# Attention and two expert layers on one core: transposes and the last queries' scores through two row halves of the array, operands without shifted columns

## The chip, the cores and the metric

The kernel runs on one core of a Trainium2 chip. The metric is the device time of one execution in microseconds (us), the median of the runs. The core has a matrix engine (TensorE; PE in the profile, and PEld for its weight loads), VectorE (DVE), ScalarE (ACT), GpSimd (POOL) and a sync engine whose queue (SP) issues all DMAs. TensorE reads SBUF and writes PSUM banks of 512 float32 columns.

## What is computed

```python
def _attn_ref(q, k, v):                       # (4, 8, 576, 64) each: 32 heads
    q_rot, k_rot = (rotate(q), rotate(k))     # rotary tables cos, sin over 576 positions
    scores = scale * np.matmul(q_rot, k_rot.transpose(0, 1, 3, 2))
...
    attn = np.exp(scores)
    attn = attn / (np.sum(attn, axis=-1, keepdims=True) + 1e-09)
    return np.matmul(attn, v).astype(np.float32)
...
    h = x @ w_in                              # layer 1: (2304, 512) @ (512, 2048), float64 weights
    g = P / (Q + 1e-06)                       # a rational function of h
    return (g @ w_out).astype(np.float32)
...
    h = np.maximum(x @ w_in, 0.0)             # layer 2
    return (h * h @ w_out).astype(np.float32)
```

## The kernel before

**Two stages.** The attention works on 16 pairs of heads; the two heads of a pair lie in the two halves of the 128 partitions (64 features each). The two expert layers follow (3840 matrix products of 464 or 456 columns). Nearly every product is made of three float32r products (high by high, low by high, high by low), for precision.

**One pair of heads.** `rope` loads q and k with their swapped halves (`raw`), multiplies by the tables, adds (POOL, for the first pairs DVE), splits into a high part (`hi`, a cast on ACT) and a low part (`lo`, POOL). `scores` computes, for each of five groups of queries (c = 0 to 4; four of 128 and a last one of 64 for each head), products of 64 rows: head 0 in the upper row half of the array, head 1 in the lower one, side by side, into two PSUM banks `sc`. DVE takes the scaled maximum and moves the scores to `e` (one instruction, "max" below), ACT does the exponential. TensorE transposes `e` in pieces of 128 x 128 (`move`; 41 in a pair) into one of two PSUM banks `tr`, alternately; ACT or DVE copies them to `et` ("eth"). `av` multiplies `et` by v with 64 output columns for each head, the heads in the two column halves of the array, in float32 (each product stands as two instructions in the trace), for the queries of c = 0, 1 (256 columns) and c = 2, 3, 4 (320). DVE copies the result to `t`; `normalise` forms the reciprocal sums, sends them through DRAM (`dr`, `rr`), and POOL multiplies (`fin`).

Before the change every q and k operand has 640 columns (`W`), head 0 shifted by 64: in this layout the last 64 queries of both heads make one product of full height with `qt` (four small ACT casts, "wrap", build it), so its scores come in one bank and one max.

**The order.** All work is recorded as tasks with an engine, an estimated duration, a rank and its reads and writes. `Plan.run` deals them out: on each engine it takes, of the tasks that are ready by its estimates, the one with the lowest rank (the position in the program plus an entry of the table `RANK`). The result is a fixed order of instructions on each engine, and each engine executes its own in order, waiting on semaphores. TensorE tasks carry a mode, rows, columns or full, by the part of the array that they use; the planner charges a change of mode (`SWITCH`).

**Weights of the layers.** Float64 words are turned into float32 pairs by `Weights.chunk`, on DVE three instructions ("wy") for each chunk of 512 columns. Seven chunks are prepared during the attention, in the pairs from the fourth to the tenth.

Of the kernel before, what the change touches and what calls it, by code (L numbers as in the profile page):

```python
# [19 lines left out]
P = 128  # L20
B, H, S, D = 4, 8, 576, 64
NPAIR = B * H // 2
W = S + D
# [16 lines left out]
CUT = 192  # L40
KCUT = 352
# [49 lines left out]
class Plan:  # L91
# [38 lines left out]
    def run(self, trace=True):  # L130
# [41 lines left out]
SWITCH, BOND = 160, 56.5  # L172

RANK = {"const": -298.5, "load": -213.6, "rope": 80.3, "add": -79.5, "hi": 153.2, "lo": -107.5,
        "wrap": 223.7, "spread": -16.2, "vload": -129.4, "qk": -228.9, "max": -56.4, "exp": 149.9,
        "dup": 356, "tr": -129, "trc": -323.5, "eth": -52.9, "av": 224.5, "t": -2.5, "inv": 97,
        "fin": -180.1, "wload": 342.6, "wx": 198.5, "wy": 82.9, "wh": 310.7, "wl": -189.1, "xh": 498.3,
        "xl": 83.4, "h": -171.3, "chain": 19.2, "gh": -121.9, "gl": 471.2, "o": 216.6, "evac": 21.5,
        "out": -157}
# [55 lines left out]
class Attention(Ops):  # L235


    def __init__(self, nc, plan, early, late, scores, banks, dram, qk, v, tables, ident, xf):
# [4 lines left out]
        self.ntr = self.ny = 0  # L243
        self.tab = early.tile([P, 2, W], F32, "tab")
        self.raw = early.tile([P, 4, W], F32, "raw")
        two = lambda shape, t: [a.tile([P] + shape, F32R, f"{t}{i}") for i, a in enumerate((early, late))]
        self.qh, self.ql, self.kh, self.kl = (two([W], t) for t in ("qh", "ql", "kh", "kl"))

        self.qt = two([2, P], "qt")
# [9 lines left out]
    def constants(self):  # L259
        for i, cols in enumerate((slice(0, KCUT), slice(KCUT, W))):  # L260
            self.dma((40 * i, "const"), self.tab[:, :, cols], self.tables_ap[:, :, cols], w=[("tab", i)], ns=900)
        self.dma((90, "const"), self.ident, self.ident_ap, w=["ident"])
        for i in range(2):
            for x, key in ((self.qt[i][0:64, :, 64:128], ("zero", i, 0)), (self.qt[i][64:128, :, 0:64], ("zero", i, 1))):
                self.fill("pool", 200, (20, "const"), f(x), 0.0, r=["early"], w=[key])

    def rotate(self, p, j, cols, pieces, rank, eng, r=()):

        raw, n = self.raw, cols.stop - cols.start
        two, w = slice(2 * j, 2 * j + 2), [("raw", j, i) for i in pieces]  # L270
        self.tt(eng[0], 2 * n, (rank, "rope"), raw[:, two, cols], raw[:, two, cols], self.tab[:, :, cols], ALU.mult,
                r=[("tab", 0), ("tab", 1)][cols.start >= KCUT:2 if cols.stop > KCUT else 1] + ["early", *r], w=w)
        self.tt(eng[1], n, (rank, "add"), raw[:, 2 * j, cols], raw[:, 2 * j, cols], raw[:, 2 * j + 1, cols], ALU.add,
                r=["early"], w=w)

    def rope(self, p):
# [3 lines left out]
        up, dn = slice(0, 64), slice(64, 128)  # L280

        def prepare(j, cols, pieces, rank):

            n = cols.stop - cols.start
            first = p == 0
# [3 lines left out]
            engines = {0: ("dve", "dve") if j else ("pool", "pool"), 1: ("dve", "dve")}.get(p, ("pool", "pool"))  # L289
            self.rotate(p, j, cols, pieces, rank, engines)  # L290
            src = raw[:, 2 * j, cols]
            self.hi("act", n, (rank, "hi"), hi[:, cols], src, r, wh)
# [3 lines left out]
        if p == 0:  # L296
            prepare(1, slice(0, KCUT), (0,), at - 50)
            prepare(0, slice(0, CUT), (0,), at - 40)
            prepare(1, slice(KCUT, W), (1,), at - 30)
            prepare(0, slice(CUT, W), (1,), at - 9)  # L300
        else:
            prepare(0, slice(0, W), (0, 1), at)
            prepare(1, slice(0, W), (0, 1), at + KFIRST)
        for i, part in enumerate(parts[0]):
            for rows, dst in ((up, slice(0, 64)), (dn, slice(64, 128))):
                self.act(64, (at, "wrap"), self.qt[b][rows, i, dst], f(part[rows, S:W]), r=["early", (names[0][i], b, 1)],
                         w=[("qt", b, i, rows.start)], sb=True)
        self.dma((at, "vload"), self.vst[b], self.v[p], r=["early"], w=[("v", b)])

    def hi(self, eng, n, rank, out, src, r, w):  # L310
        if eng == "act":
            self.act(n, rank, out, src, r=r + ["early"], w=w, sb=True)
        else:
            self.ts("dve", n, rank, out, src, 1.0, None, ALU.mult, r=r + ["early"], w=w)

    def scores(self, p, c):

        b, n = p % 2, 9 * p + 2 * c
        qh, ql, kh, kl, qt = (x[b] for x in (self.qh, self.ql, self.kh, self.kl, self.qt))
        rd = [(x, b, i) for x in ("kh", "kl") for i in range(2)] + ["early", "scores"]  # L320
        if c == 4:
            rd += [("zero", b, i) for i in range(2)] + [("qt", b, i, j) for i in range(2) for j in (0, 64)]
            jobs = [(0, slice(0, P), [(qt[:, 0], kh), (qt[:, 1], kh), (qt[:, 0], kl)])]
        else:
            at = slice(128 * c + 64, 128 * c + 192)
            rd += [(x, b, i) for x in ("qh", "ql") for i in range(2) if p or (i == 0 and c == 0) or (i == 1 and at.stop > CUT)]

            jobs = [(h, slice(64 * h, 64 * h + 64), [(qh[:, at], kh), (ql[:, at], kh), (qh[:, at], kl)]) for h in range(2)]

        def product():  # L330
            for i in range(3):
                for j in range(2):
                    for h, rows, terms in jobs:
                        w, k = terms[i]
                        first = (0 if c < 4 and h else 64) + 288 * j
                        self.mm(self.sc[h][:, j, 0:288], w[rows], k[rows, first:first + 288], i == 0, i == 2)

        self.pe(6 * 131, (n, "qk"), product, r=rd, w=[("sc", h) for h, _, _ in jobs], mode="full" if c == 4 else "rows")

    def unit(self, p, u):  # L340
        n = 9 * p + u
        b = p % 2
        c, h = divmod(u, 2)
        slot = (5 * p + c) % NE
        e, sc = self.e[slot], self.sc[h]
        if h == 0:
            self.scores(p, c)
        if u == 0:
            self.fill("pool", 70, (n - 1, "qk"), self.sums[b], 1.0, w=[("sums", b)])
        col = 5 * h + c if u < 8 else 4  # L350
        neg, sums = self.neg[b][:, col:col + 1], self.sums[b][:, col:col + 1]

        self.ts("dve", 2 * 288, (n, "max"), e[:, h].rearrange("p (j k) -> p j k", j=2), sc[:, :, 0:288], -SCALE, None,
                ALU.mult, op1=ALU.min, accum_out=neg, ns=760, ps=True, r=[("sc", h), "scores"], w=[("neg", b, col), ("e", slot, h)])
        self.act(S, (n, "exp"), e[:, h], e[:, h], func=AF.Exp, sb=True, bias=neg, scale=-1.0, accum_out=sums,
                 r=[("neg", b, col), ("sums", b)], w=[("e", slot, h), ("sum", b, col)])
        if u == 8:
            self.act(64, (n, "dup"), e[:, 1, 0:64], e[:, 0, 512:576], r=[("e", slot, 0)], w=[("e", slot, 1)], sb=True)

        part = 0 if c < 2 else 1  # L360
        cols = slice(128 * (c % 2), 128 * (c % 2) + 128)
        self.move([(e[:, h, 128 * k + 64 * h:128 * k + 64 * h + 128], k) for k in range(4)], (n, "tr"), [("e", slot, h)],
                  [((lambda t: t), lambda z: z[:, 4 * h:4 * h + 4, cols], 512, (part, "m", u))] if u < 8 else
                  [((lambda t: t.rearrange("p k (h q) -> p k h q", h=2)),
                    lambda z: z[:, 0:8, 256:320].rearrange("p (h k) q -> p k h q", h=2), 512, (1, "m", 8))], p, part)
        mid = lambda s: self.e[s].rearrange("p h k -> p (h k)")[:, 512:640]
        if u in (3, 7):
            prev = (slot + NE - 1) % NE
            self.move([(mid(prev), 0), (mid(slot), 1)], (n, "trc"), [("e", x, y) for x in (prev, slot) for y in (0, 1)],
                      [((lambda t: t[:, 0:2]), lambda z: z[:, 8, 0:256].rearrange("p (c q) -> p c q", c=2), 256, (part, "c"))], p, part)  # L370
        if u == 8:
            self.move([(mid(slot), 0)], (n, "trc"), [("e", slot, 0), ("e", slot, 1)],
                      [((lambda t, s=s: t[s, 0, s]), lambda z, s=s: z[s, 8, 256:320], 64, (1, "d", s.start))
                       for s in (slice(0, 64), slice(64, 128))], p, 1)

    def move(self, blocks, at, r, outs, p, part):
        i = self.ntr % len(self.tr)
        self.ntr += 1
# [7 lines left out]
        for src, dst, n, key in outs:  # L386
# [340 lines left out]
```

## Time and profile before

| | |
|---|---|
| median of 3 runs | 1102.25 us (1099.67 to 1103.45) |
| the profiled execution | 1099.96 us, span 1098.2 us |
| attention, to the first product of the layers | about 280 us |
| PE busy, share of the span | 1071.5 us, 98% |
| DVE / ACT / POOL busy | 786.8 (72%) / 644.3 (59%) / 554.5 us (50%) |
| chain that ended last | PE 94%, DVE 3%, ACT 1% |

A busy PE is not PE at its peak: ends of products are modelled and overlap. Whether PE sets the pace is read from the chain, and what a product costs from the distance of the starts of equal products.

### The profile page before, as it was taken

What the parts mean: (1) busy time and instruction counts of PE and PEld (TensorE: products, weight loads), DVE (VectorE), ACT (ScalarE), POOL (GpSimd) and SP (SyncE); (2) the same over time, 40 slices, a digit from 0 to 9 for tenths busy, and PEclk for the clock granted to TensorE, in tenths of its full rate; (3) what the DMA queues carried; (4) which work ended last, traced back from release to release, by engine and by line L of the source; (5) the groups of instructions that cost most, each with busy time, mean ns of one, the idle gap of its engine ahead of it and who ended that gap; (6) DMA issues with size and microseconds to landing.
All of it is one profiled execution on the core that took longest, in us unless ns stands there. A gap on an engine that the chain in (4) does not pass through costs nothing.

```text
span 1098.2 us, 16333 instructions
## 1 busy us (share of the span) xinstructions
PE 1071.5 (98%) x6000; PEld 900.2 (82%) x6000; DVE 786.8 (72%) x1439; ACT 644.3 (59%) x1283; POOL 554.5 (50%) x435
## 2 busy tenths in 40 slices
PE   4999999999799999999999999999999999999998
PEld 3666666666588888888888888888888888888887
DVE  6789888777898879988998999753254447435334
ACT  4888988787767877676676776453352234223221
POOL 3889999881478868876777776220020012001000
PEclk9999999999999999999999999999999999999999
DMA  4364554431001112101111100231031013000002
GB/s 151 116 199 132 166 155 129 144 109 36 12 20 47 50 58 59 39 20 58 39 41 40 56 1 20 73 101 39 1 96 39 20 39 96 1 20 1 35 35 104
DMA packets 25537, 71.25 MB, mean 65 GB/s; under 512 B 5104, under 2 KB 9328, under 8 KB 25456
## 3 DMA queue, kind: packets, MB, share of 16 engines
q1 hardware_dynamic: 25456, 70.20, 20.9%
q8 instruction: 47, 0.77, 0.3%
q14 instruction: 34, 0.28, 0.1%
HBM read 65.21 MB, written 4.98 MB: 64 GB/s over the span
## 4 chain that ended last, share of the span: by engine, by line
PE 94%; DVE 3%; ACT 1%; DMA 0%; issue 0%; SPq 0%; DVEq 0%; ACTq 0%
PE bank L232 44%; PE ph L232 36%; PE bank L383 8%; PE sc L232 7%; DVE raw L208 0%; DMA raw<-in_qk 0%; DVE xl L208 0%; DVE xf L208 0%; ACT e L198 0%; DVE tt L208 0%; DVE wy L213 0%; DVE u L213 0%; ACT xh L196 0%; ACT et L196 0%; SPq L229 0%
## 5 line engine op out<-in xcount | busy, mean ns | idle before, releaser
L232 PE MATMUL ph<-xh,wsi 128*128 128x464 f32 (+1 forms) x680 | 198.5, 373 | 4.5 <-DVE g L213 4.5
L232 PE MATMUL bank<-gh,wso 128*128 128x464 f32 (+1 forms) x680 | 197.6, 372 | 0.0
L196 ACT CAST gh<-g 128x464 fp32r<-128x464 f32 (+1 forms) x160 | 91.9, 576 | 153.8 <-PE bank L232 141.1
L232 PE MATMUL ph<-xh,wli 128*128 128x464 f32 (+1 forms) x600 | 174.2, 371 | 0.1
L232 PE MATMUL bank<-gh,wlo 128*128 128x464 f32 (+1 forms) x600 | 174.3, 371 | 0.0
L208 DVE TENSOR_TENSOR gl<-g,gh 128x464 fp32r<-128x464 f32 (+1 forms) x80 | 51.7, 647 | 142.5 <-ACT gh L196 142.4
L232 PEld LDWEIGHTS ph<-xh,wsi 128*128 128x128 f32 x680 | 128.1, 189 | 20.9 <-ACT xh L196 4.9
L232 PEld LDWEIGHTS bank<-gh,wso 128*128 128x128 f32 x680 | 127.6, 188 | 14.8 <-DVE xf L208 0.3
L218 DVE TENSOR_SCALAR_CACHE_REDUCE e<-sc 128x576 f32<-128x576 f32 x144 | 105.2, 755 | 40.4 <-PE sc L232 39.7
L232 PE MATMUL ph<-xl,wsi 128*128 128x464 f32 (+1 forms) x340 | 127.0, 374 | 1.6 <-DVE xl L208 1.5
L232 PE MATMUL bank<-gl,wso 128*128 128x464 f32 (+1 forms) x340 | 126.5, 372 | 0.0
L232 PEld LDWEIGHTS ph<-xh,wli 128*128 128x128 f32 x600 | 112.3, 188 | 14.2 <-DVE g L213 0.8
L232 PEld LDWEIGHTS bank<-gh,wlo 128*128 128x128 f32 x600 | 112.6, 188 | 12.9
L208 POOL TENSOR_TENSOR gl<-g,gh 128x464 fp32r<-128x464 f32 (+1 forms) x80 | 103.5, 1295 | 26.1 <-ACT gh L196 25.2
L198 ACT ACTIVATE e<-e,neg 128x576 f32<-128x576 f32 x144 | 111.1, 775 | 7.6 <-DVE e L218 6.9
L232 PE MATMUL bank<-gl,wlo 128*128 128x464 f32 (+1 forms) x300 | 111.6, 372 | 0.0
L232 PE MATMUL ph<-xl,wli 128*128 128x464 f32 (+1 forms) x300 | 111.4, 371 | 0.0
L208 POOL TENSOR_TENSOR u<-u,ab 128x464 f32<-128x464 f32 (+1 forms) x80 | 105.1, 1316 | 1.9
L383 PE MATMUL bank<-ident,e 128*128 128x128 f32 x656 | 98.0, 285 | 1.0 <-ACT et L196 0.8
L208 DVE TENSOR_TENSOR xf<-bank,xf 128x464 f32<-128x464 f32 (+1 forms) x120 | 74.4, 634 | 31.5 <-PE bank L232 30.0
L232 PE MATMUL bank<-et,vst 128*64 128x256 f32 (+1 forms) x640 | 96.8, 420 | 0.1
L198 ACT ACTIVATE tt<-ph 128x464 f32<-128x464 f32 (+1 forms) x80 | 44.4, 555 | 87.8 <-DVE g L208 72.5
(76 smaller groups left out, 1989.3 us busy)
## 6 DMA issues: line engine op xcount, KB each, us to landing
raw<-in_qk SPq DMA_DIRECT2D x30, 640.0 KB
rawi<-in_wi SPq DMA_DIRECT2D x32, 512.0 KB
rawo<-in_wo SPq DMA_DIRECT2D x32, 512.0 KB
vst<-in_v SPq DMA_DIRECT2D x16, 320.0 KB
rr<-dr SPq DMA_DIRECT2D x32, 144.0 KB
out<-xf SPq DMA_DIRECT2D x12, 232.0 KB
out<-xf SPq DMA_DIRECT2D x8, 228.0 KB
raw<-in_qk SPq DMA_DIRECT2D x1, 448.0 KB
```

Of the source, the lines that this page charges most:

```text
L196: self.nc.scalar.copy(ap(out), ap(src))
L198: self.nc.scalar.activation(ap(out), ap(src), func, **{k: ap(x) for k, x in kw.items()})
L208: self.plan.add(eng, ns, rank, lambda: self.engine(eng).tensor_tensor(ap(out), ap(a), ap(b), op=op), r, w, shared=not ps)
L218: self.plan.add(eng, ns, rank, lambda: self.engine(eng).tensor_scalar(ap(out), ap(a), ap(s0), ap(s1), op0=op0, **{k: ap(x) for k, x in kw. ...
L232: self.nc.tensor.matmul(ap(out), ap(w), ap(x), start=start, stop=stop)
L383: self.nc.tensor.transpose(ap(tr[:, k]), ap(src), ap(self.ident))
```

## The change

Transposes take 64 partitions of `e` at a time: the upper half goes through the upper row half of the array into the first `tr` bank, the lower half through the lower row half into the second, two at a time, each with 64 columns of the identity. Both banks belong to one `move`. The copies to `et` are split in the same way (`EVAC` puts six of eight large ones on ACT). q and k have 576 columns, `qt` and its casts are gone. The scores of the last 64 queries go through the row halves too: head 0 as a product of 64 rows by 64 columns, head 1 as one of 64 rows by 128 columns, of which the upper 64 results are used; they need both banks and two maxima of 64 partitions. `t` is copied in one piece for both heads; the reciprocals of head 1 come in two DMAs. All entries of `RANK` are new, so the order changes everywhere, in the layers too.

```diff
-CUT = 192
-KCUT = 352
+CUT = 128
+KCUT = 288
+TRANSPOSE = 60
+ROPE = {(0, 0): "pool", (0, 1): "dve", (1, 0): "dve", (1, 1): "dve"}
+EVAC = {("m", c, r): "act" for c in range(4) for r in range(2) if (c, r) not in ((1, 1), (2, 1))}
...
-SWITCH, BOND = 160, 56.5
+SWITCH, BOND = 160, 77.2
...
-        self.raw = early.tile([P, 4, W], F32, "raw")
+        self.raw = early.tile([P, 4, S], F32, "raw")
...
-            jobs = [(0, slice(0, P), [(qt[:, 0], kh), (qt[:, 1], kh), (qt[:, 0], kl)])]
...
+            at = slice(128 * c, 128 * c + 128) if c < 4 else slice(S - P, S) if h else slice(S - 64, S)
+            jobs.append((slice(64 * h, 64 * h + 64), slice(0, at.stop - at.start), [(qh[:, at], kh), (ql[:, at], kh), (qh[:, at], kl)]))
...
-        tr, et = self.tr[i], self.et[part][p % 2]
+        et = self.et[part][p % 2]
 
         def transposes():
-            for src, k in blocks:
-                self.nc.tensor.transpose(ap(tr[:, k]), ap(src), ap(self.ident))
-
-        self.pe(109.5 * len(blocks), at, transposes, r=r + ["ident"], w=[("tr", i)])
+            for k, pair in enumerate(zip(*halves)):
+                for i, src in enumerate(pair):
+                    rows = slice(64 * i, 64 * i + 64)
+                    src = ap(src)
+                    self.nc.tensor.transpose(ap(self.tr[i])[0:src.shape[1], 64 * k:64 * k + 64], src[rows], ap(self.ident)[rows, rows])
+
+        self.pe(TRANSPOSE * len(halves[0]), at, transposes, r=r + ["ident"], w=[("tr", i) for i in range(2)], mode="rows")
...
-            self.take("dve", m, (at, "t"), self.t[own, o:o + m], y[own, a:a + m], r=[yk], w=[("t", h, o)])
+        self.take("dve", n, (at, "t"), self.t[:, 256 * part:256 * part + n], y[:, 0:n], r=[yk], w=[("t", part)])
```

Two places of the new order matter below. The first is DVE at the turn from pair 12 to pair 13, before (`e<-sc` is a max, `et<-bank` a copy of transposes, `t<-bank` a copy of the product with v):

```order
L218 TENSOR_SCALAR e_93,neg_97<-sc_125 128x576
L218 TENSOR_SCALAR e_93,neg_97<-sc_126 128x576
L397 COPY et_108<-bank_65 64x64 x2
L432 STREAM_TRANSPOSE rt_104<-r_102 128x32
L218 TENSOR_SCALAR e_94,neg_97<-sc_125 128x576
L218 TENSOR_SCALAR e_94,neg_97<-sc_126 128x576
L397 COPY t<-bank_66 64x256 x2
L218 TENSOR_SCALAR e_95,neg_97<-sc_125 128x576
L218 TENSOR_SCALAR e_95,neg_97<-sc_126 128x576
```

The same turn on DVE in the changed kernel, the maxima of c = 0, of c = 1 and of c = 2:

```order
L220 TENSOR_SCALAR e_93,neg_97<-sc_123 128x576
L220 TENSOR_SCALAR e_93,neg_97<-sc_124 128x576
L385 COPY et_106<-bank_64 128x2x64
L385 COPY et_106<-bank_65 128x2x64
L385 COPY et_106<-bank_64 128x4x64
L385 COPY et_106<-bank_65 128x4x64
L385 COPY et_106<-bank_64 64x64
L220 TENSOR_SCALAR e_94,neg_97<-sc_123 128x576
L220 TENSOR_SCALAR e_94,neg_97<-sc_124 128x576
L385 COPY et_106<-bank_65 64x64
L385 COPY t<-bank_66 128x256
L220 TENSOR_SCALAR e_95,neg_97<-sc_123 128x576
```

Five copies of the pair before now stand between the maxima of c = 0 and of c = 1, where two small copies stood. In the same stretch TensorE has the scores of c = 1 and of c = 2 directly behind each other (24 products in a row, as at 12 places of the attention), and the first transposes of the pair behind them.

The second place is TensorE at the scores of the last queries, before:

```order
L383 MATMUL bank_65<-ident,e_94 128x128 x4
L232 MATMUL bank_67<-et_107,vst_121 64x320 x2
L232 MATMUL sc_125<-kh_88,qt_90 128x288 x4
L232 MATMUL sc_125<-kl_89,qt_90 128x288 x2
L383 MATMUL bank_64<-ident,e_94 128x128 x4
L383 MATMUL bank_65<-ident,e_95 128x128 x4
```

And in the changed kernel (the pair of rows with 64x288 and 128x288 comes six times, with `ql` and `kl` too):

```order
L234 MATMUL bank_67<-et_106,vst_119 64x320 x4
L372 MATMUL bank_64<-ident,e_95 128x64
L372 MATMUL bank_65<-ident,e_95 128x64
L372 MATMUL bank_64<-ident,e_92 128x64
L372 MATMUL bank_65<-ident,e_92 128x64
L234 MATMUL bank_67<-et_106,vst_119 64x320 x2
L234 MATMUL sc_123<-kh_88,qh_86 64x288
L234 MATMUL sc_124<-kh_88,qh_86 128x288
```

Six products of full height became six pairs in the row halves, and their outputs alternate between 64 and 128 partitions. Over the whole attention TensorE's order changes mode (rows, columns, full) 254 times before and 144 times after, the step into the layers included.

## Rows read from the trace of the kernel before

**Rows 1.** Busy time of each engine, attention and layers (windows).

```profile
core 0: us, PE busy (x) PEld busy (x) DVE busy (x) ACT busy (x) POOL busy (x), PEclk, DMA share, GB/s
40.00:277.00 237.00, 236.82 (x1977) 160.15 (x1977) 193.24 (x492) 197.06 (x479) 193.18 (x114) 1.00 0.44 132
300.00:1098.00 798.00, 793.65 (x3786) 709.89 (x3784) 549.07 (x868) 407.25 (x720) 331.12 (x290) 1.00 0.14 43
```

**Rows 2.** The chain that ended last, 199 to 232 us: start, length, what.

```profile
by line: PE bank L383 35.1%; PE bank L232 35.0%; PE sc L232 30.0%
...
199.74 1.66 PE bank L232 x12
201.40 0.99 PE sc L232 x12
...
215.71 1.66 PE bank L232 x12
```

**Rows 3.** Weight loads of the last queries' scores, once in each pair (timeline).

```profile
76.55 0.56 PEld L232 LDWEIGHTS sc<-kh,qt 128*128 128x128 f32 x4 [0.49 <-DVE et L397]
...
191.14 0.56 PEld L232 LDWEIGHTS sc<-kh,qt 128*128 128x128 f32 x4 [0.49 <-DVE et L397]
...
207.05 0.56 PEld L232 LDWEIGHTS sc<-kh,qt 128*128 128x128 f32 x4 [0.49 <-DVE et L397]
...
223.02 0.56 PEld L232 LDWEIGHTS sc<-kh,qt 128*128 128x128 f32 x4 [0.49 <-DVE et L397]
```

**Rows 4.** TensorE in one pair (timeline).

```profile
201.33 0.30 PEld L232 LDWEIGHTS sc<-kh,qh 64*128 64x128 f32 x4 [0.49 <-DVE t L397]
...
201.71 0.43 PE L232 MATMUL sc<-kh,ql 64*128 64x288 f32 x4
...
201.97 0.42 PE L232 MATMUL sc<-kl,qh 64*128 64x288 f32 x4
202.32 0.85 PEld L383 LDWEIGHTS bank<-ident,e 128*128 128x128 f32 x8 [0.16 <-issue]
202.32 1.09 PE L383 MATMUL bank<-ident,e 128*128 128x128 f32 x8
...
203.35 1.30 PE L232 MATMUL bank<-et,vst 128*64 128x320 f32 x8
...
206.37 0.76 PE L232 MATMUL bank<-et,vst 128*64 128x320 f32 x4
...
213.04 0.66 PE L383 MATMUL bank<-ident,e 128*128 128x128 f32 x4
```

**Rows 5.** VectorE in the same stretch (timeline).

```profile
202.43 0.76 DVE L218 TENSOR_SCALAR_CACHE_REDUCE e<-sc 128x576 f32<-128x576 f32 x1 [1.13 <-PE sc L232]
203.11 0.08 DVE L218 DVE_READ_ACCUMULATOR e<-sc 128x1 f32 x1
203.11 0.75 DVE L218 TENSOR_SCALAR_CACHE_REDUCE e<-sc 128x576 f32<-128x576 f32 x1
203.79 0.08 DVE L218 DVE_READ_ACCUMULATOR e<-sc 128x1 f32 x1
...
206.35 0.42 DVE L397 COPY et<-bank 128x256 f32<-128x256 f32 x1
...
206.69 0.75 DVE L218 TENSOR_SCALAR_CACHE_REDUCE e<-sc 128x576 f32<-128x576 f32 x1
...
212.75 0.45 DVE L397 COPY et<-bank 64x64 f32<-64x64 f32 x2
```

**Rows 6.** A wait of TensorE for DVE in the first pair (timeline).

```profile
26.93 0.08 DVE L218 DVE_READ_ACCUMULATOR e<-sc 128x1 f32 x1
...
27.07 0.98 PEld L232 LDWEIGHTS sc<-kh,qt 128*128 128x128 f32 x4 [2.41 <-DVE e L218]
```

**Rows 7.** Groups between 70 and 268 us (by line and form): busy, mean ns.

```profile
L198 ACT ACTIVATE e<-e,neg 128x576 f32<-128x576 f32 x111 | 85.7, 775 | 5.2 <-DVE e L218 4.8
...
L208 POOL TENSOR_TENSOR raw<-raw,tab 128x1280 f32<-128x1280 f32 x22 | 65.0, 2968 | 1.8 <-DMA raw<-in_qk 1.6
...
L213 DVE SCALAR_TENSOR_TENSOR wy<-wx,wy 128x512 uint32<-128x512 uint32 x7 | 5.7, 813 | 0.2
...
L218 DVE TENSOR_SCALAR wy<-rawi 128x512 uint32<-128x512 uint32 x4 | 4.5, 1132 | 0.0
...
L213 DVE SCALAR_TENSOR_TENSOR wy<-rawi,wy 128x512 uint32<-128x512 uint32 x4 | 3.7, 915 | 0.0
```

More of the change, by code (lines that the diff above doesn't have):

```diff
@@ L171 @@
 SAME, CROSS = 130, 180
-SWITCH, BOND = 160, 56.5
[L174 to L179, printed above, removed]
+SWITCH, BOND = 160, 77.2
+RANK = {"const": -332.5, "load": -240.8, "rope": 66.7, "add": -190.1, "hi": 466.7, "lo": -245, "wrap": 223.7,
+        "spread": -16.2, "vload": -62.2, "qk": 7.4, "max": -58.9, "exp": 101.9, "dup": 356, "tr": -448.9,
+        "trc": 381.9, "eth": -54.1, "av": 438, "t": 370.8, "inv": 804, "fin": -323.6, "wload": 966,
+        "wx": 467.4, "wy": 51.1, "wh": 143.9, "wl": -174.2, "xh": 554.7, "xl": 53.4, "h": -384.7,
+        "chain": -206.7, "gh": -85.2, "gl": 575.4, "o": 40.3, "evac": -273.4, "out": -182.5}
 class Ops:
@@ L259, in constants @@
     def constants(self):
-        for i, cols in enumerate((slice(0, KCUT), slice(KCUT, W))):
+        for i, cols in enumerate((slice(0, KCUT), slice(KCUT, S))):
             self.dma((40 * i, "const"), self.tab[:, :, cols], self.tables_ap[:, :, cols], w=[("tab", i)], ns=900)
         self.dma((90, "const"), self.ident, self.ident_ap, w=["ident"])
[L263 to L274, printed above, removed]
     def rope(self, p):
@@ L332, in product @@
                 for j in range(2):
-                    for h, rows, terms in jobs:
+                    for h, (rows, m, terms) in enumerate(jobs):
                         w, k = terms[i]
[L335 to L341, printed above, removed]
+                        self.mm(self.sc[h][m, j, 0:288], w[rows], k[rows, 288 * j:288 * j + 288], i == 0, i == 2)
@@ L342, in unit @@
+        self.pe(6 * 131, (n, "qk"), product, r=rd, w=[("sc", h) for h in range(2)], mode="rows")
+    def unit(self, p, c):
+        n = 9 * p + 2 * c
         b = p % 2
-        c, h = divmod(u, 2)
         slot = (5 * p + c) % NE
[L345 to L348, printed above, removed]
+        e, ek = self.e[slot], [("e", slot, h) for h in range(2)]
+        if c == 0:
             self.fill("pool", 70, (n - 1, "qk"), self.sums[b], 1.0, w=[("sums", b)])
-        col = 5 * h + c if u < 8 else 4
@@ L351, in unit @@
[L351 to L374, printed above, removed]
@@ L389, in eth @@
-    def eth(self, n, cols):
-        return "act" if cols == 512 and n % 9 not in (2, 5) else "dve"
+        self.scores(p, c)
+        every = slice(0, P)
+        for h, rows, i, col in [(0, every, 0, c), (1, every, 1, 5 + c)] if c < 4 else [(h, slice(64 * h, 64 * h + 64), 1, 4) for h in range(2)]:
+            self.ts("dve", 2 * 288, (n + h, "max"), e[rows, i].rearrange("p (j k) -> p j k", j=2), self.sc[h][rows, :, 0:288],
+                    -SCALE, None, ALU.mult, op1=ALU.min, accum_out=self.neg[b][rows, col:col + 1], ns=760, ps=True,
+                    r=[("sc", h), "scores"], w=[("neg", b, col, h), ("e", slot, h)])
+            if c < 4 or h:
+                self.act(S, (n + h, "exp"), e[:, i], e[:, i], func=AF.Exp, sb=True, bias=self.neg[b][:, col:col + 1],
+                         scale=-1.0, accum_out=self.sums[b][:, col:col + 1],
+                         r=[("neg", b, col, x) for x in (range(2) if c == 4 else (h,))] + [("sums", b)],
+                         w=[("e", slot, x) for x in (range(2) if c == 4 else (h,))] + [("sum", b, col)])
@@ new lines, in unit @@
+        part = c // 2 if c < 4 else 1
+        q = 128 * (c % 2)
+        flat = lambda s: self.e[s].rearrange("p h k -> p (h k)")
+        blocks = lambda s, i, h: [self.e[s][:, i, 128 * k + 64 * h:128 * k + 64 * h + 128] for k in range(4)]
+        mid = lambda s: flat(s)[:, 512:640]
+        prev = (slot + NE - 1) % NE
+        every8 = lambda x: x.rearrange("p (k q) -> p k q", q=64)
+        if c < 4:
+            src = blocks(slot, 0, 0) + blocks(slot, 1, 1)
+            self.move([src, src], (n + 1, "tr"), ek,
+                      [(r, every, slice(0, 512), lambda z, r=r: z[:, 0:8, q + 64 * r:q + 64 * r + 64], ("m", c, r)) for r in range(2)], p, part)
@@ new lines, in unit @@
+        mids = [(r, every, slice(0, 128), lambda z, r=r: z[:, 8, 0:256].rearrange("p (c q) -> p c q", c=2)[:, :, 64 * r:64 * r + 64],
+                 ("c", r)) for r in range(2)]
+        if c == 1:
+            both = [mid(prev), mid(slot)]
+            self.move([both, both], (n + 1, "trc"), [("e", prev, h) for h in range(2)] + ek, mids, p, part)
+        if c == 4:
+            prev2 = (slot + NE - 2) % NE
+            both = [mid(prev2), mid(prev)]
+            last = [e[:, 1, 512:576], mid(slot)]
+            own = [slice(64 * r, 64 * r + 64) for r in range(2)]
+            self.move([both + blocks(slot, 1, r) + [last[r]] for r in range(2)], (n, "trc"),
+                      [("e", s, h) for s in (prev2, prev, slot) for h in range(2)],
+                      mids + [(r, every, slice(128, 384), lambda z, r=r: z[:, 4 * r:4 * r + 4, 256:320], ("m", 4, r)) for r in range(2)] +
+                      [(r, own[r], slice(384, 448), lambda z, r=r: z[own[r], 8:9, 256:320], ("d", r)) for r in range(2)], p, 1)
@@ new lines, in move @@
+    def move(self, halves, at, r, outs, p, part):
+        et = self.et[part][p % 2]
+        def transposes():
+            for k, pair in enumerate(zip(*halves)):
[4 more added lines that the diff above has]
+        self.pe(TRANSPOSE * len(halves[0]), at, transposes, r=r + ["ident"], w=[("tr", i) for i in range(2)], mode="rows")
+        for i, rows, cols, dst, key in outs:
+            n = cols.stop - cols.start
+            self.take(EVAC.get(key, "dve"), n, (at[0], "eth"), dst(et), self.tr[i][rows, cols].rearrange("p (k q) -> p k q", q=64),
+                      r=[("tr", i)], w=[("et", p % 2, part) + key])
@@ L406, in av @@
         self.ny += 1
-        keys = [("et", b, part, "m", x) if isinstance(x, int) else ("et", b, part, "d", int(x[1:])) if x[0] == "d"
-                else ("et", b, part, "c") for x in us]
+        keys = [("m", c, r) for c in ((0, 1), (2, 3, 4))[part] for r in range(2)] + [("c", r) for r in range(2)]
+        keys = [("et", b, part) + k for k in keys + [("d", r) for r in range(2)] * part]
         def product(js):
@@ L447, in build @@
         for p in range(NPAIR):
-            for u in range(9):
-                self.unit(p, u)
-                if u == 3:
+            for c in range(5):
+                self.unit(p, c)
+                if c == 1:
                     self.av(p, 0)
@@ L626, in build @@
         ps = ctx.enter_context(tc.tile_pool(name="ps", bufs=1, space=PSUM))
-        banks = [ps.tile(s, F32, name=f"bank{i}") for i, s in enumerate([[P, 4, P]] * 2 + [[P, 512]] * 2)]
+        banks = [ps.tile([P, 512], F32, name=f"bank{i}") for i in range(4)]
         xf = base.tile([P, NDM, NT], F32, name="xf")
```

77 lines of the change are left out of this document (24 added, 53 removed).

## Prediction

> **What bounds the kernel now.** I read the windows first [rows 1]: in the attention PE is busy in all of 237 us, DVE, ACT and POOL in 193 to 197; in the layers PE is busy in 793.65 of 798 us. Since a busy PE need not be the bound, I then read the chain that ended last for two pairs of heads [rows 2]: it runs through nothing but TensorE, 35.1% transposes, 35.0% products with v, 30.0% scores. The pace of the pairs is the distance of the same weight load in neighbouring pairs [rows 3]: 223.02 - 207.05 = 15.97 us in a light pair, and (191.14 - 76.55) / 7 = 16.37 us in the seven heavy ones, in which DVE also unpacks weights. The layers' products stay as they are and leave 4 us of idle PE in 798, so only the attention and the step out of it can give anything.
>
> **What a pair costs TensorE today** [rows 4]. Eight transposes take 1.09 us and four 0.66, so one is (1.09 - 0.66) / 4 = 0.108 us; 41 make 4.4 us. Four instructions of the product with v over 320 columns, two side by side, are worth 1.30 - 0.76 = 0.54, so a pass of 320 columns is 0.27 us (0.84 ns a column); five passes of two instructions for 320 columns and for 256 (0.216 each) make 2.7 + 2.16 = 4.85. Scores: 201.97 - 201.71 = 0.26 for two pairs of row halves, 0.13 a pair of 288 columns; five groups of six make 3.9. The sum is 13.2. The pair takes 15.97; the missing 2.8 us go to some 16 changes of mode (254 in 16 pairs), 0.17 us each, which is also the idle time in front of the first weight load of the transposes [rows 4].
>
> **Part 1: the transposes.** 128 columns in 0.108 us are 0.84 ns a column, exactly the rate of the float32 product with v, so I take a transpose to be bound by its moving columns. With 64 columns it is 0.054, with the few ns between instructions 0.057 us for both halves together. That the halves run together is what the scores show: the four weight loads of two row halves start within 0.30 us, four full ones need 0.56 [rows 3, 4]. 41 steps then cost 2.3 us instead of 4.4. The bounds: 0.108 if the halves take turns or the weight load sets the pace (nothing gained), and 0.054 below.
>
> **Part 2: modes.** 144 changes instead of 254: 9 a pair, 1.5 us instead of 2.7. Scores of the last queries: six pairs at 0.13 for six full products at 0.13, nothing. So TensorE's need falls from 15.97 to about 3.9 + 2.3 + 4.85 + 1.5 = 12.6 us. If it stayed the bound, the kernel would gain 3.3 us in 16 pairs, 53 us.
>
> **Part 3: what is late next.** Both banks of `sc` now belong to every group, both banks of `tr` to every move, and DVE gets a tenth max and split copies. I walk through one light pair by the new order, with times from the rows. A max starts 1.10 us after the first weight load of its scores (201.33 to 202.43) [rows 4, 5], of which 0.11 is the load, hidden when transposes stand ahead. One max is 0.68 (202.43, 203.11, 203.79), a copy of 256 elements 0.34 (206.35 to 206.69), one of 64 about 0.24, one of 128 between, 0.27 [rows 5]. From the end of a max's read to the next weight load there are 0.06 (26.93 + 0.08 to 27.07) [rows 6], so 0.13 after the slot of the max.
>
> The scores of c = 0 start at 0. DVE takes their maxima from 0.98 to 2.35, then the five copies (2 x 0.27 + 2 x 0.34 + 0.24 = 1.46) to 3.81, and only then the maxima of c = 1, ready since 3.6, to 5.18. The scores of c = 2 wait for both banks, to 5.31. TensorE has nothing else in its order between c = 1 and c = 2: it is idle for 2 us here, and for half a microsecond ahead of c = 1. From 5.31 on it works without a gap to the next pair's c = 0: scores of c = 2 (0.90 with the load), c = 3, c = 4 (0.79 each), 34 transpose steps (1.9), products with v of 5 x 0.54 and 4 x 0.43 (4.4), 8 changes of mode (1.4), together 10.2. In this part every bank is free in time (c = 3 is wanted at 8.5, its banks are free at 7.9). The pair takes 5.3 + 10.2 = 15.5 us, 0.45 less than now. That is my reading of the change: nearly all of the 3.3 us that TensorE saves is spent on a wait for DVE at the start of each pair.
>
> The Trainium skill, "TensorEngine Tiling (Array Packing)", section "PSUM Bottleneck", says that tiling speeds up TensorE but not the copies out of PSUM, which may become the bottleneck. No row of the kernel before shows that, since TensorE sets its pace; by the rule alone the gain is the smaller one of the walk, not the 53 us.
>
> **Heavy pairs.** A chunk's three instructions are 1.13 + 0.92 + 0.81 = 2.9 us of DVE [rows 7]. Today they cost 16.37 - 15.97 = 0.4 a pair, since DVE waits for TensorE. In the new order one or two of them stand in the DVE stretch ahead of c = 2; the same walk gives 16.3 for one such pair and 16.8 for its neighbour, so I take 16.5, 0.15 more than now (bounds: 15.6, all hidden, and 18.4, all on the path).
>
> **Other engines.** ACT loses five small copies and one eth a pair and keeps its nine exponentials of 0.775 us; POOL's rotary work shrinks by a tenth (2.97 us multiplications [rows 7]). Both were at 13 of 16 us, so neither decides. The start, some 5 us of rotary work on DVE before the first products, loses a tenth, 0.5 us. The layers' new order can only lose, since PE is full there; I take 0 (bound 4, as much as they idle today).
>
> **Sum.** Nine light intervals (the first one, cold, among them) x -0.45 = -4.0; seven heavy x +0.15 = +1.0; start -0.5: -3.5, so 1096.5 us on the profiled execution's own time of 1099.96. That execution lies 0.2% below the median of 1102.25; on that the same saving is 1098.7. I say 1097. About 0.3%, 3.3 us, is what a measurement of this kernel can tell from no change, and my saving sits at that edge.
>
> **Rivals.**
> A. DVE catches up better than in my walk (copies cheaper, ACT taking its share earlier): the wait ahead of c = 2 halves, 1 us a pair, 16 us: about 1082. For it: DVE is busy in only 193 of 237 us [rows 1]. Against: its order is fixed, and the copies stand ahead of the maxima.
> B. The change doesn't do what it says: a transpose step costs 0.108, because the halves take turns. The 34 steps on the path cost 34 x 0.051 = 1.7 us more a pair, 28 us: about 1124. It decides from a step of 0.07 on (0.45 / 34 more than 0.057). For it: no row shows four instructions within 0.057 us for long. Against: the score halves.
> C. Slower by the mixed shapes of the last scores. 64 and 128 output columns alternate twelve times a pair. If each alternation costs what a change of mode costs now (0.17) and the halves no longer overlap (6 x 0.13), this is 2.8 us on the path of every pair, 45 us: about 1142. For it: from full to column halves (`bank<-ident` to `bank<-et,vst`) only the columns change, and there too the chain has its 0.17. Against: both are row-half products in one stream, and the hardware may use the full width for both. It decides from 0.04 us per alternation.
> The Trainium skill, same page, section "Key Properties", has a rule that stands for C: changing the tiling mode, not just the tile, drains TensorE. No run here shows whether 64 x 64 next to 64 x 128 counts as such a change.
> D. Heavy pairs, or the layers' new order, cost more than I take: heavy pairs at 17.5 instead of 16.5 and 2 us in the layers, 9 us: about 1106. DVE in the first layer is as full as in the attention and its order is new.
>
> **Chances.** My walk 0.50, A 0.14, B 0.10, C 0.10, D 0.16. The walk alone spans 1091 to 1103 (0.35 us a pair either way, the latencies' uncertainty), so faster by over 0.3% is A and 0.6 of the walk, 0.44; slower is B, C, D's larger part and a little of the walk, 0.30; the same 0.26. The range for 8 in 10 reaches from 1085, well into A, to 1124, B's time; C and the far side of A stay outside.
>
> **What would show it.** Right: transposes of 64 columns that start 0.057 us apart in pairs; the chain of the attention no longer all TensorE but with DVE's maxima and copies of `et` ahead of c = 1 and c = 2; weight loads of scores idle for some 2 us once a pair behind a max; light pairs 15.5 apart. Wrong in step 1: distance 0.1. Rival C: the last queries' scores of a pair take 3 us instead of 0.8. Rival D: intervals of the heavy pairs above 17, or PE idle in the layers. If pairs come 14 us apart, my walk misjudged DVE.

## The result: 0.9% slower, because the new waits let TensorE's clock fall

The changed kernel takes 1111.13 us (median of 12 runs, 1103.69 to 1115.98), the kernel before 1102.19 (12 runs); the ratio is 1.0091, 95% interval 1.0069 to 1.0113. The forecast was 1097 with "faster" as the likeliest sign. The profiled execution is the longest of the twelve, 1115.98 us, span 1114.2.

The windows of the profile after, columns as in [rows 1]: the attention, the layers, then two neighbouring light pairs (from the last queries' scores of one pair to those of the next) and a stretch of the second one.

```profile
core 0: us, PE busy (x) PEld busy (x) DVE busy (x) ACT busy (x) POOL busy (x), PEclk, DMA share, GB/s
40.00:277.00 237.00, 213.58 (x2525) 150.10 (x2521) 197.64 (x499) 165.74 (x369) 170.44 (x111) 0.92 0.39 122
300.00:1114.00 814.00, 805.97 (x3836) 720.71 (x3834) 558.09 (x893) 419.49 (x740) 341.34 (x299) 1.00 0.14 42
...
203.84:219.95 16.11, 14.34 (x185) 9.82 (x183) 13.33 (x35) 11.52 (x27) 12.35 (x8) 1.00 0.39 115
219.95:236.84 16.89, 15.62 (x184) 10.86 (x182) 13.11 (x35) 11.56 (x27) 12.29 (x8) 0.90 0.37 110
...
229.14:232.56 3.42, 3.42 (x33) 2.71 (x33) 2.34 (x8) 1.91 (x5) 3.42 (x3) 0.50 0.03 5
```

The reader is to see two things. TensorE, busy in all of the attention before [rows 1], now stands idle for 23 us of 237. And the granted clock, 1.00 there before, is 0.92: in the second pair it is 0.50 (1.2 GHz) for 3.42 us. The trace has twelve such stretches, 51 us in all, eleven of them in the attention; the kernel before has two, at its start and at the turn to the layers.

The chain that ended last, 199 to 232 us (start, length, what):

```profile
203.91 1.02 PE sc L234 x12
...
206.63 0.88 ACT e L200 x2
...
207.53 1.48 DVE r L220
...
209.04 0.36 DVE r L415
...
210.21 0.76 DVE e L220 x3
210.97 1.19 DVE et L385 x5
212.15 1.36 DVE e L220 x4
...
213.56 0.98 PE sc L234 x11
214.54 0.57 PE bank L372 x15
...
224.04 0.88 PE sc L234 x12
...
226.40 1.06 PE sc L234 x11
...
228.13 0.76 DVE e L220 x3
...
228.94 1.52 PE sc L234 x11
```

Where [rows 2] showed nothing but TensorE, the chain now leaves it. In the first of the two pairs it is away from 204.9 to 213.56: ACT's work with the exponential of the last queries, the sums' reciprocal, the maxima of c = 0, the five copies of `et`, the maxima of c = 1, then the scores of c = 2. In the second pair it is away twice for 1.5 us, for the maxima of c = 0 (224.9 to 226.40) and for those of c = 1 (227.46 to 228.94). The copies and maxima are the stretch that the forecast walked through; the reciprocal ahead of them in the first pair (L220 and L415 on `r`) is not in it.

TensorE in the first pair, and its two longest waits in the second (timeline, answers to [rows 4]):

```profile
203.84 0.55 PE L234 MATMUL sc<-kh,qh 64*64 64x288 f32 x4
...
204.41 0.50 PE L234 MATMUL sc<-kl,qh 64*64 64x288 f32 x4
...
210.34 0.40 PE L234 MATMUL sc<-kh,qh 64*128 64x288 f32 x1 [0.40 <-DVE e L220]
211.02 0.53 PE L234 MATMUL sc<-kh,qh 64*128 64x288 f32 x3 [0.28 <-DVE e L220]
...
212.88 0.39 PE L234 MATMUL sc<-kh,qh 64*128 64x288 f32 x1 [0.80 <-DVE e L220]
213.56 0.53 PE L234 MATMUL sc<-kh,qh 64*128 64x288 f32 x3 [0.29 <-DVE e L220]
...
216.27 0.71 PE L372 MATMUL bank<-ident,e 64*128 64x64 f32 x16
216.79 0.51 PE L234 MATMUL sc<-kh,qh 64*128 64x288 f32 x4
...
228.26 0.40 PE L234 MATMUL sc<-kh,qh 64*128 64x288 f32 x1 [0.81 <-DVE e L220]
228.94 0.69 PE L234 MATMUL sc<-kh,qh 64*128 64x288 f32 x3 [0.28 <-DVE e L220]
```

Eight steps of transposes take 216.79 - 216.27 = 0.52 us, 0.065 a step of two halves: forecast 0.057, before 0.108. The last queries' scores are done in 0.8 us. The waits for DVE are there, 0.40 + 0.28 ahead of c = 1 and 0.80 + 0.29 ahead of c = 2. The second pair has less of them, 0.18 and 0.81 + 0.28, yet it is the second in which the clock falls, at 229.14, right behind the last of them.

VectorE and POOL in the same place (two timelines):

```profile
207.53 1.47 DVE L220 TENSOR_SCALAR r<-sums 128x32 f32<-128x32 f32 x1 [0.38 <-ACT e L200]
209.04 0.35 DVE L415 RECIPROCAL r<-r 128x32 f32<-128x32 f32 x1
...
209.56 0.72 DVE L220 TENSOR_SCALAR_CACHE_REDUCE e<-sc 128x576 f32<-128x576 f32 x1
...
274.64 0.18 DVE L220 TENSOR_SCALAR r<-sums 128x32 f32<-128x32 f32 x1 [0.27 <-ACT e L200]
```

```profile
207.53 1.44 POOL L210 TENSOR_TENSOR kl<-raw,kh 128x576 fp32r<-128x576 f32 x1
```

The same addition to 32 sums takes 0.18 us when POOL is idle and 1.47 when it starts together with POOL's subtraction; it ends when that ends. (Before the change its mean was already 738 ns; now it is 998.) The unpacking of the weights also gets longer beside POOL. Its two slowest groups (30 to 295 us, busy and mean ns), first before, then after:

```profile
L218 DVE TENSOR_SCALAR wy<-rawo 128x512 uint32<-128x512 uint32 x3 | 3.2, 1075 | 0.0
L213 DVE SCALAR_TENSOR_TENSOR wy<-rawo,wy 128x512 uint32<-128x512 uint32 x3 | 3.1, 1018 | 0.0
```

```profile
L215 DVE SCALAR_TENSOR_TENSOR wy<-rawo,wy 128x512 uint32<-128x512 uint32 x3 | 5.8, 1931 | 0.0
L220 DVE TENSOR_SCALAR wy<-rawo 128x512 uint32<-128x512 uint32 x3 | 5.3, 1763 | 0.0
```

All `wy` instructions together take 25.3 us in the seven chunks, before 20.2. The Trainium skill, "Trainium Architecture — The Big Picture", section "What this means for kernel authors", says that DVE and GpSimd share an SBUF port under an exclusive lock; the rows of the addition agree (0.18 us alone, 1.47 beside POOL).

### The profile page after: what moved, and what is told of

Its sections match the earlier page's. It is cut to its first block, busy times and chain, and to the rows that moved or that the text cites. A ratio compares the mean times of both kernels' runs of the same rounds, so it can differ in the third digit from the quotient of the medians.

```text
span 1114.2 us, 17891 instructions
## 1 busy us (share of the span) xinstructions
PE 1061.9 (95%) x6752; PEld 901.6 (81%) x6752; DVE 794.3 (71%) x1487; ACT 621.8 (56%) x1187; POOL 535.3 (48%) x431
## 4 chain that ended last, share of the span: by engine, by line
PE 87%; DVE 8%; issue 2%; DMA 1%; ACT 1%; POOL 1%; SPq 0%; DVEq 0%; ACTq 0%; POOLq 0%
PE bank L234 42%; PE ph L234 35%; PE sc L234 6%; DVE e L220 4%; PE bank L372 3%; DVE et L385 1%; DMA raw<-in_qk 1%; DVE r L220 1%; POOL raw L210 0%; ACT e L200 0%; DVE wy L215 0%; SPq L231 0%; DMA cols<-in_b 0%; DVE xl L210 0%; POOL ql L210 0%
## 5 line engine op out<-in xcount | busy, mean ns | idle before, releaser
L220 DVE TENSOR_SCALAR_CACHE_REDUCE e<-sc 128x576 f32<-128x576 f32 (+1 forms) x160 | 115.5, 751 | 26.9 <-PE sc L234 22.7
L210 POOL TENSOR_TENSOR u<-u,ab 128x464 f32<-128x464 f32 (+1 forms) x80 | 100.1, 1254 | 3.3
L234 PE MATMUL bank<-et,vst 128*64 128x256 f32 (+1 forms) x640 | 100.4, 440 | 0.9 <-DVE et L385 0.9
L234 PE MATMUL sc<-kh,qh 64*128 64x288 f32 (+1 forms) x320 | 60.6, 379 | 37.7 <-DVE e L220 25.1
```

The source lines that it names most:

```text
L210: self.plan.add(eng, ns, rank, lambda: self.engine(eng).tensor_tensor(ap(out), ap(a), ap(b), op=op), r, w, shared=not ps)
L220: self.plan.add(eng, ns, rank, lambda: self.engine(eng).tensor_scalar(ap(out), ap(a), ap(s0), ap(s1), op0=op0, **{k: ap(x) for k, x in kw. ...
L234: self.nc.tensor.matmul(ap(out), ap(w), ap(x), start=start, stop=stop)
```

## The experiments

Theory K: the waits came as priced, and the loss is TensorE's clock after them. Theory W: the clock is a symptom, DVE's stretch itself grew beyond the walk (the addition that waits for POOL, the unpacking).

**Work for TensorE in its waits** (e1_fill). Transposes of the identity, read by nobody:

```diff
+FILL = {1: 2, 2: 5}
...
         def product():
+            for _ in range(FILL.get(c, 0) if p else 0):
+                self.nc.tensor.transpose(ap(self.y[1])[:, 320:448], ap(self.ident), ap(self.ident))
```

> The changed kernel, and in each pair but the first TensorE does two more whole-array transposes of the identity ahead of the scores of c = 1 and five ahead of those of c = 2, into columns of a PSUM bank that nobody reads. They wait for nothing and lie where TensorE waits for DVE: 7 x 0.108 us and their changes of mode are about 1.4 us a pair, against waits of 0.4 + 0.28 and 0.8 + 0.29 us in the pair at 207 to 224 us. DVE, ACT and POOL do what they did. Theory K (clock): the waits for DVE that the prediction priced came as priced, and what turned the forecast round is that TensorE's granted clock falls to 1.2 GHz after such waits, twelve stretches of 51 us in the profiled run. Then no such stretch is left between 40 and 290 us, the mean clock is above 0.993 and the time is 1094 to 1102. Theory W (waits): the clock is a symptom, the time is lost in DVE's stretch itself, which got longer than priced. Then the clock may rise, but the time stays at 1108 to 1118.

Measured: 1102.82 us, ratio 1.0012 (1.0000 to 1.0023), clock 0.994. The windows, and TensorE in a pair (timeline):

```profile
40.00:277.00 237.00, 224.33 (x2744) 156.56 (x2740) 202.94 (x526) 174.46 (x390) 171.93 (x112) 0.99 0.39 123
226.97:242.30 15.33, 14.83 (x189) 10.54 (x189) 12.57 (x34) 11.02 (x26) 12.09 (x8) 1.00 0.38 121
```

```profile
233.00 0.44 PE L310 MATMUL bank<-ident 128*128 128x128 f32 x2
233.38 1.03 PE L235 MATMUL sc<-kh,qh 64*128 64x288 f32 x4
...
234.86 0.77 PE L310 MATMUL bank<-ident 128*128 128x128 f32 x5
235.74 0.39 PE L235 MATMUL sc<-kh,qh 64*128 64x288 f32 x1
236.41 0.54 PE L235 MATMUL sc<-kh,qh 64*128 64x288 f32 x3 [0.28 <-DVE e L221]
```

The wait of 0.80 us ahead of c = 2 is filled, the clock stays at 2.4 GHz in this pair (in the attention two stretches of 3.4 us at 1.2 GHz are left of eleven; theory K had expected none), and 8.3 us of the median come back though TensorE does more. Theory W's 1108 is excluded; K's range is missed by 0.8 us at its upper end.

**The same work elsewhere** (e7_fill_elsewhere): `FILL = {3: 2, 4: 5}`, into the other idle bank.

> The changed kernel with the same seven extra transposes a pair, but two ahead of the scores of c = 3 and five ahead of those of c = 4, where TensorE has no wait to fill. Theory K: the waits stay empty, TensorE falls to 1.2 GHz after them as before (some ten stretches between 40 and 290 us), and the seven transposes with their changes of mode, about 1.2 us, add to most pairs: 1118 to 1135. If it is only the amount of TensorE's work that counts and not where it lies, the clock stays at 0.993 or above and the time is that of the changed kernel less the clock's loss plus the work, 1110 to 1120.

Measured: 1122.9 us, ratio 1.0192 (1.0177 to 1.0208), clock 0.986.

```profile
40.00:277.00 237.00, 215.30 (x2518) 149.13 (x2516) 192.26 (x482) 161.28 (x359) 169.40 (x110) 0.95 0.38 120
```

The time lies in theory K's range. Outside the waits the work adds to the pairs, and the clock still falls, though less often (0.95 instead of 0.92 in the attention, with six stretches). So where the work lies matters; whether its amount counts for something too, one profiled run does not show.

**Without the addition to the sums** (e2_no_add), and with the fill (e6_fill_no_add, where the reciprocal stands in the addition's place; in e2_no_add it keeps its own place, which in six pairs lies behind the reset of the sums for a later pair, so that it reads reset sums there). The edit of e2_no_add:

```diff
-        self.ts("dve", 32, at, r, self.sums[b], 1e-9, None, ALU.add,
-                r=[("sum", b, i) for i in range(9)] + [("sums", b)], w=[("r", b)])
-        self.plan.add("dve", 270, at, lambda: self.nc.vector.reciprocal(ap(r), ap(r)), w=[("r", b)])
+        self.plan.add("dve", 84.7, at, lambda: None, r=[("sum", b, i) for i in range(9)] + [("sums", b)], w=[("r", b)], shared=True)
+        self.plan.add("dve", 270, at, lambda: self.nc.vector.reciprocal(ap(r), ap(self.sums[b])), w=[("r", b)])
```

> The changed kernel without the addition of 1e-9 to the sums (the reciprocal reads the sums themselves); the order of everything else is kept. In the changed kernel this addition of 32 columns takes 0.18 us when POOL is idle and 1.0 to 1.5 us where a subtraction of POOL runs at the same time, and in about half the light pairs it stands directly ahead of the maxima of c = 0. Theory W: it is what made the walk too short; 0.5 to 1.2 us a pair come back, 8 to 16 us in all, 1095 to 1103, and the clock rises with the shorter waits. Theory K: only the 0.5 us by which an undisturbed pair missed the walk (16.07 instead of 15.5) in some of the pairs; the waits between c = 1 and c = 2 stay and most stretches at 1.2 GHz with them: 1103 to 1109.

> The filled kernel of the first experiment (1102.82 us, clock 0.994), and the reciprocal reads the sums themselves in the place where 1e-9 was added, so the addition of 32 columns is left out; everything else keeps its order. It prices, with the clock held up, the addition that waits for POOL (1.0 to 1.5 us instead of 0.18 in most pairs). If the addition stands on the path: light pairs all at 15.4 (they are 15.37 to 16.09 in the filled kernel), heavy ones up to 1 us shorter, 5 to 10 us in all, 1093 to 1098. If the fill has already hidden it, since the maxima of c = 0 wait elsewhere: 1101 to 1103.

Measured: 1107.64 us, ratio 1.0069 (1.0038 to 1.0101), without the fill; 1101.78, ratio 1.0003 (0.9991 to 1.0016), with it. One light pair of each in the windows, first without the fill, with its stretch at the lower clock, then with it:

```profile
224.50:241.40 16.90, 15.64 (x186) 10.75 (x184) 12.45 (x37) 11.63 (x27) 12.25 (x9) 0.90 0.34 110
224.66:228.08 3.42, 3.42 (x32) 2.52 (x31) 2.18 (x7) 2.07 (x5) 3.42 (x3) 0.50 0.03 5
```

```profile
224.00:239.40 15.40, 15.00 (x195) 10.44 (x193) 11.99 (x35) 11.54 (x27) 12.43 (x9) 1.00 0.43 138
```

This is the cleanest price of the clock: a light pair takes 16.90 us with one stretch at 1.2 GHz and 15.40 without, 1.5 us, nearly half of 3.42 (the two light pairs of e2_no_add without a stretch, and without fill, take 15.37 and 15.36). The addition itself is worth little: where it stands on the path a light pair is 0.5 to 0.7 us longer (15.9 in the filled kernel and 16.1 in the changed one instead of 15.4), but with the fill only 1.0 us of the whole comes back, which the intervals of the two ratios do not tell from nothing (the profiled clock is 0.992 there, 0.994 in the filled kernel). It was theory W's main cause, and it falls: 1107.64 lies in K's range, not in W's.

**Without the unpacking** (e3_no_unpack), and the same with the fill (e5_fill_no_unpack): for the first six of seven chunks DVE's three `wy` instructions are not issued.

> The changed kernel without DVE's unpacking of the weights in the first six chunks (three instructions of 512 columns each are left out, their weights are zero; the order of the rest is kept). In the changed kernel these instructions take 0.42 and 0.68 us when alone and up to 2.5 and 3.0 us where POOL works. Rival D (heavy pairs): pairs with unpacking fall from 17 to 19 us to the 16 of light ones, 12 to 18 us in all, 1094 to 1099. Theory K alone: the unpacking lies mostly beside other waits, 2 to 6 us, 1105 to 1109, and stretches at 1.2 GHz remain about as many.

> The filled kernel without DVE's unpacking of the weights in the first six chunks (their weights are zero; the order of the rest is kept). It prices the heavy pairs with the clock held up: in the filled kernel the pairs with unpacking stand 16.1 to 18.6 us apart, light ones 15.4 to 15.9. Rival D: the excess goes, 10 to 14 us, 1089 to 1093. If the excess came from something else that is left, for example POOL's subtraction for the weights or ACT's casts: less than half of it, 1097 to 1102.

Measured: 1106.22 us, ratio 1.0051 (1.0034 to 1.0069), and with the fill 1097.15, ratio 0.9960 (0.9944 to 0.9976). The first lies in theory K's range for it and outside rival D's, with twelve stretches at the lower clock as in the changed kernel. The second is 5.7 us less than the filled kernel and lies at the lower end of the second expectation, 1097 to 1102, not in rival D's. In the profiled executions, 3.7 us apart, the seven heavy intervals take 118.3 us instead of 120.1, so 1.8 us of the saving lies in them. Two of the seven are long in either kernel: 18.41 and 18.37 us in the filled one, 18.13 and 18.97 without the unpacking. Each of these four holds a stretch at 1.2 GHz; in the filled kernel they are

```profile
79.81:83.23 3.42, 3.42 (x33) 2.74 (x33) 3.42 (x9) 1.95 (x5) 3.42 (x4) 0.50 0.90 259
148.08:151.49 3.41, 3.41 (x35) 2.72 (x33) 3.41 (x8) 2.58 (x6) 3.41 (x3) 0.50 0.45 134
```

The other five heavy intervals average 16.7 us with the unpacking and 16.2 without it. So the unpacking is worth about 0.4 us a pair, and the two longest pairs are long through the clock; what else keeps heavy pairs above light ones is not shown.

**The old table on the new structure** (e4_old_table): `RANK` and `BOND` of the kernel before.

> The changed kernel with the kernel before's table of ranks and its bond, so that the new structure is ordered by the old preferences. If the new table is the culprit (a bad order laid over a good structure), the time falls below 1102. If the order of the changed kernel is fitted to its structure and the loss lies in the structure (two banks for every group of scores, ten maxima on DVE), the old table makes it worse: pairs of 16.8 to 21 us, 1125 to 1145.

Measured: 1135.47 us, ratio 1.0303 (1.0282 to 1.0324). The new table is no culprit against the old one.

**Another order** (e8_order), with the fill (e9_order_fill), and its two settings without its table (e10_copies):

```diff
-EVAC = {("m", c, r): "act" for c in range(4) for r in range(2) if (c, r) not in ((1, 1), (2, 1))}
-AVCUT = ((0, 1), (2, 3), (4,))
+EVAC = dict.fromkeys([("c", 0), ("m", 0, 0), ("m", 0, 1), ("m", 1, 0), ("m", 1, 1), ("m", 2, 0), ("m", 2, 1), ("m", 3, 0), ("m", 3, 1), ("m", 4, 1)], "act")
+AVCUT = ((0, 1), (2,), (3,), (4,))
...
+SAME1, CROSS1 = 108, 142
...
+FIRST = {"const": 2209.6, "load": -3748.5, "rope": 644.1, "add": -2457.2, "hi": 1678.4, "lo": -3052.9, "vload":
...
+        ns *= self.cost.get(rank[1], 1)
+        rank = self.base + rank[0] + self.table[rank[1]]
```

> The changed kernel's structure with another order of the attention: its own table of ranks and estimates for the attention's tasks, the products with v cut into finer tasks (so that their last pieces can stand in TensorE's waits for DVE), and the layers keep their table. By a walk with the changed kernel's durations, pairs of 15.5 with the clock held up become 14.5 to 15.7, heavy ones too; two waits of about 0.9 us a pair are left on TensorE. From the heavy and the first pair's excess (about 6 us over the forecast) and 0.5 us a light pair some 13 us come back: with the clock at 1.0 that is 1087 to 1092. Theory K: the waits that are left let the clock fall as often as in the changed kernel, or half as often: 1091 to 1101. If the order does not matter and the structure with two banks for every group bounds the pair: 1105 to 1115 as before.

> The kernel of the new order with extra whole-array transposes of the identity in its two longest waits of a pair (one and four in the first nine pairs, four and five after), into columns of a PSUM bank that is idle. Theory K: the clock is at 0.994 or above and the time 1086 to 1094, by at least 2 us under the same order without them. If the extra work does not fit the waits (each transposes' group brings two changes of mode of 0.17 us): above the same order without them.

> The changed kernel with two settings of the faster order alone: the copies of the transposes as they are split there (ten pieces on ACT instead of six; DVE keeps four) and the product with v cut into finer tasks; table, bond and estimates are those of the changed kernel. If the gain of the faster order (1090.1 us) came from the load taken off DVE: 1088 to 1097. If it needs the order that its table makes: the pairs stay uneven at 15.4 to 21 us by a walk with the clock held up, TensorE waits for DVE and its clock falls: 1102 to 1115.

Measured: e8_order 1090.1 us, ratio 0.9895 (0.9880 to 0.9911), clock 0.998; e9_order_fill 1091.09, 0.9904 (0.9891 to 0.9918); e10_copies 1108.43, 1.0064 (1.0041 to 1.0086). The attention's window of e8_order, then of e10_copies:

```profile
40.00:277.00 237.00, 223.02 (x2717) 150.06 (x2714) 179.20 (x468) 206.06 (x486) 178.62 (x117) 1.00 0.40 126
```

```profile
40.00:277.00 237.00, 216.00 (x2572) 145.40 (x2569) 173.95 (x444) 191.59 (x451) 174.18 (x112) 0.96 0.39 122
```

Both take some 20 us of load off DVE, but only the one with the new table keeps the clock at 1.00 and is fast, so the order is needed (whether it would do without these copies, no run shows). Its pairs, heavy ones too, stand 15.2 to 15.5 us apart from the third to the twelfth interval (the last three 15.9 to 16.8); TensorE still waits in them, for example

```profile
175.40 0.40 PE L245 MATMUL sc<-kh,qh 64*128 64x288 f32 x1 [1.08 <-DVE e L231]
176.08 0.53 PE L245 MATMUL sc<-kh,qh 64*128 64x288 f32 x3 [0.28 <-DVE e L231]
...
248.31 0.53 PE L245 MATMUL sc<-kh,qh 64*128 64x288 f32 x3 [0.40 <-DVE e L231]
...
255.24 0.40 PE L245 MATMUL sc<-kh,qh 64*128 64x288 f32 x1 [0.67 <-DVE e L231]
```

but without a fall of the clock, where theory K had expected at least half as many falls as in the changed kernel. So the fill, where no loss is left to cure, gains nothing, again against what theory K expected. This version beats both kernels: 1.05% faster than before.

## Why the prediction was wrong

The sum of the forecast (which counted nine light intervals; there are eight with the first, so its terms add up to -3.1) beside the filled kernel, which has the changed kernel's order with the clock nearly held up (profiled executions, against before; intervals as in [rows 3]):

| term | forecast, us | measured, us |
|---|---|---|
| 7 light intervals | -0.45 each | -0.35 each, -2.5 |
| first interval | -0.45 | +1.0 (18.59, before 17.62) |
| 7 heavy intervals | +0.15 each, +1.0 | +0.79 each, +5.5 (17.2 on average; 16.7 without the two that hold a stretch at 1.2 GHz) |
| start, to the first pair's last scores | -0.5 | -1.2 (25.84, before 27.07) |
| step into the layers | 0 | +1.0 |
| layers and end | 0 | -1.5 |
| all of these | -3.5 | +2.3 |
| TensorE at 1.2 GHz, net of what the fill costs (medians: 1111.13 - 1102.82) | none | +8.3 |

**The step that failed** is the second half of the walk: "From 5.31 on it works without a gap to the next pair's c = 0 [...] together 10.2". Its durations came from a kernel in which TensorE never waited in a pair and the clock was at 1.00. I priced the wait as the time it takes, 2 us, and not for what it does to the work behind it. In the pairs in which the clock falls, the work costs 1.5 us more, and the saving of 0.45 a pair is gone three times over. The warning lay in rows that I had quoted for another purpose: in [rows 6] four weight loads of the last queries' scores take 0.98 us behind a wait of 2.41, in [rows 3] the same four take 0.56. The window there, in the kernel before:

```profile
26.98:30.39 3.41, 3.32 (x14) 3.10 (x14) 2.43 (x8) 2.25 (x7) 1.92 (x2) 0.50 0.73 203
```

No rival of mine had this mechanism. The Trainium skill, "TensorE: Matmul & The Clock Gate", section "A second HAM failure mode: psum-queue depth-cycling", describes a kernel that idles for short moments between groups as it cycles through PSUM banks, and whose clock swings between its two levels. The rows agree for the pair whose clock falls at 229.14, with waits of 0.18, 0.81 and 0.28 us; the pair before it, with 0.40 + 0.28 + 0.80 + 0.29 us, kept its clock.

**Part 1** was right: 0.065 us a step, halves side by side, and rival B (0.108) is out. **Part 2** was right, and rival C is out: 0.8 us for the last queries' scores, no drain between 64 and 128 columns. **Part 3**, the wait between c = 1 and c = 2, was right in place and, at 2.4 GHz, in the length of the pair: light pairs of 15.4 to 15.9 us with the fill and 16.1 without it, forecast 15.5. The wait ahead of c = 2 was smaller than the 2 us of the walk: 0.80 and 0.29 us, with one product of 0.39 between them. The walk left out the addition and the reciprocal of the sums that stand ahead of the maxima of c = 0 in some pairs (the 15.9 and 16.1), worth 1 us in all by e6_fill_no_add. Rival A's pairs, 1 us shorter than the walk, came neither in the changed kernel nor in the filled one.

**Heavy pairs** look mis-sized: 16.5 forecast, 17.2 measured in the filled kernel and 17.5, rival D's figure, in the changed one. But in the changed kernel the four that hold a stretch at 1.2 GHz take 18.1 to 19.1 us and the other three 15.6 to 16.5, and in the filled kernel the five without a stretch average 16.7. So the forecast was nearly right for 2.4 GHz, and D's figure came from the clock, not from D's cause. A chunk's three instructions did grow, from 2.9 us to 3.6 in the changed kernel, but leaving them out brought only 0.4 us a pair. Rival D's loss in the layers did not come. The first pair was not light: I counted it as one without a row for it.

So the sign was lost to the clock. Of the +2.3 in the table some 3 us belong to the two stretches left in it (an estimate, at the 1.5 us of a light pair), so that the change without any loss of clock would have saved about 1 us instead of 3.5. The twelve runs of the changed kernel point the same way: a straight line through their times and clocks (0.975 to 0.989) falls by 0.8 us for each 0.001 of clock and would reach 1099.5 us at 0.997, the clock of the kernel before; that too is an estimate, beyond the range of the runs. Two things stay open: why short waits of some kernels lower the clock and those of e8_order, one of them 1.08 us, do not (the rows show where the clock fell, not what decides it), and what keeps heavy pairs above light ones without the unpacking.

## What to carry to other kernels

A change that frees TensorE but makes it wait in short pieces must be priced twice: the wait, and the work behind it at 1.2 GHz; in this kernel the second was more than twice the forecast saving. Look for any wait that the old trace has, and read the granted clock and the same instruction's length behind it. If such waits can't be ordered away, work that nobody reads, laid into them, can hold the clock up: here it brought 8.3 us net, and nothing where the clock had not fallen. Better is another order: e8_order brought 21 us over the changed kernel.

## What the hardware showed that I had not expected

In the light pairs after 220 us no wait is longer than 0.81 us and all waits of a pair come to 1.2 to 1.4 us of 17, and still the clock fell once in each; in the profiled run TensorE ran at 1.2 GHz for 51 us in all. In e8_order a wait of 1.08 us passed without a fall. Time went with the clock: among the twelve runs the one with a mean clock of 0.989 took 1103.69 us, the one with 0.977 took 1115.98. And a DVE instruction of 0.18 us between SBUF tiles takes 1.47 when POOL's subtraction starts at the same time; the reciprocal right behind it, also between SBUF tiles, takes 0.34 to 0.35 there, and 0.34 at 229.51 beside a multiplication of POOL.
